# Layer 0's first products taken by sequence tile over all row blocks in eight PSUM banks, all in rounded parts; an own chain for the first tile; another order and other queues for the last half's stores

## The chip, the cores and the metric

The kernel runs on one core of one Trainium2 chip. The core has five engines that run side by side and meet through semaphores: TensorE (PE; PEld is its weight load), VectorE (DVE), ScalarE (ACT), GpSimd (POOL) and SyncE (SP), which here only issues DMAs. All DMAs, whichever engine issues them, are carried by the core's 16 DMA engines. The metric is the device time of one execution in microseconds (us), as the median of several runs.

## The reference

The model alternates two layers, twice. Layers 0 and 2 are a Fourier mixing layer, layers 1 and 3 a gated feed-forward layer; each is added to its input. Sequence length S is 2048, width D is 512, hidden width F is 1792, all in float32.

```python
def _A_ref(x, dft_seq_re, dft_seq_im, dft_hid_re, dft_hid_im):
    a = jnp.einsum("bsd,ed->bse", x, dft_hid_re)
    b = jnp.einsum("bsd,ed->bse", x, dft_hid_im)
    return jnp.einsum("ts,bse->bte", dft_seq_re, a) - jnp.einsum("ts,bse->bte", dft_seq_im, b)
def _B_ref(x, w_gate, w_up, w_down):
    return (_gelu(x @ w_gate) * (x @ w_up)) @ w_down
x = A_x
x = x + _A_ref(_layernorm(x), ...)
x = x + _B_ref(_layernorm(x), ...)
x = x + _A_ref(_layernorm(x), ...)
x = x + _B_ref(_layernorm(x), ...)
```

## The kernel before

**Products.** A float32 product is made of three faster matmuls. Each operand is divided into a rounded high part (ACT copies it into the type float32r) and the low rest (DVE subtracts the high part from the value); `split` does this (L115 to L117). `mm3` (L148 to L152) then adds high by high, high by low and low by high into one PSUM bank. A plain float32 matmul is used in one place only, below.

**Mixing layer.** The product with the sequence matrices comes first. The sequence is cut into four row blocks `b` of 512 output rows and 16 sequence tiles of 128 input rows; the matrix pieces `ws` are 128 by 512 and 256 KB each. Real and imaginary part form a 2 by 2 block product in Strassen's manner with seven products per row block, named A11, A12, S2, S1, S3, S4, A22. Each product runs over `NK` = 8 tiles, with two column halves `c`, so one product of one row block is 8 x 2 x 3 matmuls. `plan` (L387) lists the stages. In layer 0 the two products A11 (tiles 0 to 7 of the normalized rows, left half) and A12 (tiles 8 to 15) of all four row blocks come first: A11 for b = 0, 1, 2, 3, then A12 for b = 0, 1, 2, 3, each in two banks of its own. The remaining products of block 0 follow (S2 with S1 and S3, then S4 with A22), each with products by the hidden matrices between, then those of blocks 1, 2 and 3.

**A11 and A12.** `a11` (L733) asks `bare` (L400) whether it is layer 0, block 0. There the raw piece `t` is multiplied with the normalized row `za[k]` by two plain float32 matmuls (L739), without dividing either. Otherwise `six` (L716) takes the divided piece from the stream and makes six matmuls. At the end of A11 both banks are copied by ACT into `sums[b]`. `a12` (L750) then adds `sums[b]` and its own banks on DVE into `t`; for blocks 1 to 3 both are put away in DRAM through POOL's queue (`put_away`, L235).

**The stream.** `items` is the list of all pieces in the order of use. `load_next` (L272) issues a load on SP; `split_next` and `take` (L297) keep up to `AHEAD` = 7 pieces divided before their use (more where `stream["more"]` is set), and `RAW` = 6 loaded ahead of that. `step` (L464), called after each group of matmuls, runs one entry of `queue`; that is how normalizing and dividing the rows is laid between products. A scheduler of the framework then sets the order of instructions on each engine.

**The opening** (L1265 to L1304). `WARM` = 16 small matmuls of the identity run first (L1267). Four rows tiles `x` and four pieces are loaded in turn, and rows 0 and 1 are normalized at once (`first_norm`, `norm_terms` L482: DVE takes `bn_stats`, `bn_aggr` and adds EPS, POOL raises to -0.5 at L497, DVE makes `shift`, and ACT applies scale and shift at L526). `queue` then holds the other rows of the first half with `first_parts` (the divided left half), then `second_norm` and `second_parts` for rows 8 to 15, then `combine` and `combine_late`, which make the sums of halves that S2 and the later products need. Working tiles come from a pool of `NSLOT` = 94 slots of 128 by 512; `norm_terms` of layer 2 takes one as a place for an output that nobody reads (`junk`).

**The end** (L1231 to L1254). The last half block of layer 3 runs its down products in the order of `down_order` (L407), where the products S3 are spread between S4, and both end at about the same time. Then `last_rows` (L1193) makes A22 in two cuts of 256 columns. After each cut DVE transposes and adds into a wide tile (`turned_rows`, L220), and four stores of 128 KB go out, two from SP and two from ACT (L1209). The rows of the neighbouring group, 1 MB, are stored by POOL when S4 is done (`rows_done`, L230, issued at L231).

Of the kernel before, what the change touches and what calls it, by code (L numbers as in the profile page):

```python
# [2 lines left out]

# [50 lines left out]
def fnet_geglu(ctx: ExitStack, tc: tile.TileContext, x_in, ws, wh, whc, wgu, wdc, out):  # L54
# [15 lines left out]
    nc.vector.memset(warm, 0.0)  # L70
    nc.scalar.activation(warm, warm, AF.Gelu_apprx_tanh)

    power = cpool.tile([P, 1], F32, name="power")
    nc.vector.memset(power, -0.5)

# [37 lines left out]
        return ap.bitcast(F32)  # L113

    def split(src, hi, lo):  # L115
        nc.scalar.activation(hi, src, AF.Copy)  # L116
        nc.vector.tensor_tensor(lo, src, f32(hi), op=ALU.subtract)  # L117

    def split_slot(src):
        hi, lo = sb.get(F32R), sb.get(F32R)  # L120
# [193 lines left out]

    s1s, s2s, s3s, cs, held = {}, {}, {}, {}, {}

    def as_is(v):
        return (v,)

    def whole(*parts):  # L320
        return parts

# [64 lines left out]
    def plan(layer):  # L387

        fore, steps = FORE[layer], []
        steps += [(b, "A11") for b in range(fore)] + [(b, "A12") for b in range(fore)]  # L390
# [9 lines left out]
    def bare(layer, b, what):  # L400

        return layer == 0 and b == 0 and what == "A11"
# [12 lines left out]

    def mix_items(layer):
        def raw(make, *tiles):
            items.append((F32, tiles, make, None))

        for b, what in plan(layer):  # L420
            tiles = [[ws[(b * 2 + m) * NS + k] for k in range(NS)] for m in range(2)]
            (a11, a12), (a21, a22) = ((r[:NK], r[NK:]) for r in tiles)
            hold = b >= FORE[layer]
            if what == "A11":
                for k in range(NK):
                    raw(as_is if bare(layer, b, what) else make_a11(k) if hold else plain, a11[k])
            elif what == "A12":
                for k in range(NK):
                    raw(plain, a12[k])
            elif what == "S2":  # L430
                for i, k in skewed(3):
                    if i == 0:
                        raw(make_s2(k, b in KEEP22[layer]), a21[k], a22[k], *(() if hold else (a11[k],)))
                    else:
                        raw(make_s1(k) if i == 1 else make_s3(k))
            elif what == "S4":
                for i, k in skewed(2):
                    if i == 0:
                        raw(make_s4(k), a12[k])
                    elif b in KEEP22[layer]:  # L440
                        raw(make_a22(k))
                    else:
                        raw(plain, a22[k])
            elif what == "PAIR":
                for name, k in PAIR_ORDER:
                    items.append((F32R, (piece_of(whd, k, name),), whole, NEAR_PAIR))
            else:
                for m, c in what:
                    if layer == 0 and b == 0:
                        items.append((F32, (wh[m * ND + c],), make_hid_first(m, c), (m, c)))  # L450
                    else:
                        items.append((F32R, halves(whs[m, c]), make_hid(m, c), (m, c)))

    for layer in range(0, 4, 2):
        mix_items(layer)
        for w in range(NB // 2):
            for near, products in zip(NEAR, down_order()):
# [54 lines left out]
    def terms_ahead(layer, i, n):  # L512

        if i == 0:
            fresh["terms"] = x_load(layer, 0)
        x, junk = fresh.pop("terms"), sb.get()
# [3 lines left out]
        sb.put(x, junk)  # L520

    def normed(layer, i, mixed=False):
        x = row_of(layer, i, mixed)
# [151 lines left out]
    def mix(layer):  # L675
# [57 lines left out]
        def a11(b):  # L733
            chain = [ps8.get() for _ in range(2)]
            for k in range(NK):
                if bare(layer, b, "A11"):
                    t, = take()
                    for c in range(2):
                        nc.tensor.matmul(chain[c], za[k][:, c * P:(c + 1) * P], t, start=k == 0, stop=k == NK - 1)  # L739
# [10 lines left out]
        def a12(b):  # L750
# [4 lines left out]
            for c in range(2):  # L755
# [9 lines left out]
                else:  # L765
                    plus(v, v, side[c])
                    cs[0, c] = v
            ps8.put(*side)

        chains, sides, us, later = {}, {}, {}, {}  # L770

# [142 lines left out]
        for n, (b, what) in enumerate(plan(layer)):  # L914
            if n == len(plan(layer)) - 1:
# [2 lines left out]
                    weight_load(1)  # L918
                while queue:
                    step()  # L920
            if what in stages:
                stages[what](b)
                if what == "S4":
                    pair_member(b)
# [82 lines left out]
    def geglu(w, layer):  # L1007
# [185 lines left out]
        def last_rows():  # L1193
# [40 lines left out]
        late = down_order()[1]  # L1234
        last = layer == 3 and w == 1
        if last:
            late = late[:-NP]
        for i, (name, k) in enumerate(late):
# [35 lines left out]
            loaded.add(i)  # L1274
            fresh[i] = x_load(0, i)

    for i in range(4):
        x_ahead(i)
        load_next()

    def opening(k):

        def run():
            x_ahead(k + 2)
            if k < NK:
                first_norm(0, k)
            first_parts(k - 2)
        return run

    def second_opening(k):  # L1290
        def run():
            x_ahead(NK + k + 2)
            second_norm(0, k)
        return run

    first_norm(0, 0)
    first_norm(0, 1)
    queue.extend(opening(k) for k in range(2, NK + 2))
    for k in range(NK):
        queue += [second_opening(k), lambda k=k: second_parts(k), *([None] if k % 2 else [])]  # L1300
    for k in range(NK):
        queue += [lambda k=k: combine(k), None]
    for k in range(NK):
        queue += [lambda k=k: combine_late(k), None]  # L1304

    for layer in range(4):
        if layer % 2 == 0:
# [70 lines left out]
```

## Time and profile before

| what | value |
|---|---|
| runs | 1599.57 us median of 3 (1598.54 to 1601.11) |
| the profiled execution: its own time | 1600.61 us |
| its span, first to last instruction | 1598.8 us |
| granted TensorE clock over the span, mean | 0.999 |
| DVE / ACT / POOL busy | 77% / 53% / 14% of the span |
| DMA moved | 422.86 MB, mean 264 GB/s |

The profile is taken from one execution. A row of the timeline gives start and duration in us, engine, line, operation, what is written from what, and in brackets the idle time before it with what ended it. A row of the windows gives, for a stretch, the busy us of each engine with the number of instructions that touch it, the granted clock, the busy share of the DMA engines and GB/s. A group row gives a count, the total busy time and the mean ns of one. One plain float32 matmul shows as two records, and a float32r matmul as one. The records of successive matmuls overlap, so what a matmul costs TensorE is the distance between two starts, not its duration; the same holds for long rows of like instructions on DVE and ACT.

### The profile page before, as it was taken

The numbers are of one execution on the slowest core, as the hardware profiler recorded it, in microseconds if no ns is written. First come the engines' busy times: TensorE is split into PE (matmuls) and PEld (weight loads), VectorE is DVE, ScalarE is ACT, GpSimd is POOL, SyncE is SP. The second block draws the span as 40 slices with busy tenths as digits, with TensorE's granted clock in tenths as the row PEclk, the third lists the DMA queues.
The fourth block names the chain that finished last, engine by engine and source line by source line (L and its number), as shares of the span: only waits on it lengthen the run. The fifth ranks groups of instructions, "written<-read, shape, count | busy, mean of one in ns | idle before, by whom it ended". The sixth has DMA issues, their size and how long they took to land.

```text
span 1598.8 us, 23037 instructions
## 1 busy us (share of the span) xinstructions
PE 1588.5 (99%) x7018; PEld 1312.4 (82%) x7018; DVE 1236.6 (77%) x2148; ACT 846.0 (53%) x1664; POOL 219.5 (14%) x409
## 2 busy tenths in 40 slices
PE   9999999999999999999999999999999999999997
PEld 6888888888888888888888888888888888888886
DVE  7999989689789795665969987789985548754484
ACT  7754464445677653556777534536446535433360
POOL 2112210211455201220041000001001000000000
PEclk9999999999999999999999999999999999999999
DMA  9869986787999999995867777886998967996462
GB/s 359 292 207 329 357 269 223 247 282 253 346 342 342 308 310 306 307 350 195 274 233 255 238 261 228 273 267 211 260 341 240 292 190 227 314 283 197 126 191 53
DMA packets 276604, 422.86 MB, mean 264 GB/s; under 512 B 28864, under 2 KB 131520, under 8 KB 275456
## 3 DMA queue, kind: packets, MB, share of 16 engines
q1 hardware_dynamic: 251600, 338.26, 66.8%
q0 software_dynamic: 23792, 82.59, 14.0%
q8 instruction: 56, 0.92, 0.2%
q10 hardware_dynamic: 1088, 0.52, 0.1%
q14 instruction: 68, 0.56, 0.1%
HBM read 339.74 MB, written 81.53 MB: 263 GB/s over the span
## 4 chain that ended last, share of the span: by engine, by line
PE 95%; DMA 3%; DVE 1%; SPq 1%; issue 0%; ACT 0%; POOL 0%; POOLq 0%; ACTq 0%
PE p L150 31%; PE p L151 31%; PE p L152 31%; DMA s<-x 1%; PE p L739 1%; DMA s<-wh 1%; SPq L187 1%; DMA xwide<-x 1%; DMA s<-wb 1%; PE p L1267 0%; DVE s L117 0%; DVE s L138 0%; ACT s L504 0%; SPq L944 0%; DVE s L134 0%
## 5 line engine op out<-in xcount | busy, mean ns | idle before, releaser
L151 PE MATMUL p<-s,s 128*128 128x512 f32 (+1 forms) x2318 | 897.0, 388 | 0.0
L152 PE MATMUL p<-s,s 128*128 128x512 f32 (+1 forms) x2318 | 892.2, 388 | 0.0
L150 PE MATMUL p<-s,s 128*128 128x512 f32 (+1 forms) x2318 | 873.3, 389 | 0.4 <-ACT s L145 0.4
L116 ACT ACTIVATE s<-s 128x512 fp32r<-128x512 f32 (+1 forms) x828 | 464.6, 606 | 350.9 <-DVE s L138 144.5
L117 DVE TENSOR_TENSOR s<-s,s 128x512 fp32r<-128x512 f32 (+1 forms) x828 | 518.5, 660 | 56.5 <-ACT s L116 54.2
L150 PEld LDWEIGHTS p<-s,s 128*128 128x128 f32 x2318 | 435.4, 188 | 91.6 <-ACT s L145 1.3
L152 PEld LDWEIGHTS p<-s,s 128*128 128x128 f32 x2318 | 435.4, 188 | 89.9 <-issue 0.5
L151 PEld LDWEIGHTS p<-s,s 128*128 128x128 f32 x2318 | 435.4, 188 | 89.6 <-issue 0.7
L141 DVE TENSOR_TENSOR s<-s,p 128x512 f32<-128x512 f32 x291 | 194.9, 681 | 195.7 <-PE p L152 109.9
L138 DVE TENSOR_TENSOR s<-s,s 128x512 f32<-128x512 f32 (+1 forms) x408 | 246.3, 618 | 11.3 <-DMA s<-ws 9.0
L145 ACT ACTIVATE s<-p 128x512 f32<-128x512 f32 x240 | 140.5, 591 | 145.8 <-PE p L152 141.4
L1004 ACT ACTIVATE s<-s 128x512 f32<-128x512 f32 x112 | 70.2, 629 | 118.2 <-DVE s L141 116.8
L507 POOL TENSOR_SCALAR rstd<-rstd 128x1 f32<-128x1 f32 x48 | 16.6, 346 | 342.2 <-ACT s L506 333.4
L1018 DVE TENSOR_TENSOR s<-s,s 128x512 f32<-128x512 f32 x84 | 57.8, 688 | 1.9
L265 POOL DMA_DIRECT2D wb<-s x84 | 45.4, 543 | 91.7 <-ACT s L116 71.1
L116 ACT ACTIVATE s<-xwide 128x512 fp32r<-128x512 f32 (+1 forms) x66 | 39.7, 616 | 24.2 <-DVE xwide L138 13.8
L526 ACT ACTIVATE s<-s,shift,rstd 128x512 f32<-128x512 f32 x61 | 48.8, 807 | 6.9 <-DVE shift L498 6.6
L141 DVE TENSOR_TENSOR s<-s,s 128x512 f32<-128x512 f32 (+1 forms) x70 | 41.6, 597 | 12.0 <-issue 5.4
L117 DVE TENSOR_TENSOR s<-xwide,s 128x512 fp32r<-128x512 f32 (+1 forms) x66 | 44.1, 674 | 5.6 <-ACT s L116 5.5
L231 POOL DMA_DIRECT2D out<-wide x8 | 5.2, 655 | 290.4 <-DVE wide L141 184.3
L504 ACT ACTIVATE s<-s 128x512 f32<-128x512 f32 x45 | 28.0, 622 | 30.6 <-DMA s<-x 28.8
L231 POOL DMA_DIRECT2D x<-wide x12 | 7.8, 660 | 237.3 <-DVE wide L141 168.7
(105 smaller groups left out, 530.0 us busy)
## 6 DMA issues: line engine op xcount, KB each, us to landing
s<-ws SPq DMA_DIRECT2D x364, 256.0 KB, 5.0
s<-wb SPq DMA_DIRECT2D x294, 256.0 KB, 5.4
s<-wc SPq DMA_DIRECT2D x196, 256.0 KB, 4.3
wb<-s POOLq DMA_DIRECT2D x98, 256.0 KB, 6.0
s<-wh SPq DMA_DIRECT2D x85, 256.0 KB, 5.3
xwide<-ws SPq DMA_DIRECT2D x55, 256.0 KB, 4.2
s<-x SPq DMA_DIRECT2D x54, 256.0 KB, 4.7
wc<-s POOLq DMA_DIRECT2D x49, 256.0 KB, 5.6
```

Source lines behind the costliest of these rows:

```text
L116: nc.scalar.activation(hi, src, AF.Copy)
L117: nc.vector.tensor_tensor(lo, src, f32(hi), op=ALU.subtract)
L138: nc.vector.tensor_tensor(out, a, b, op=ALU.subtract)
L141: nc.vector.tensor_tensor(out, a, b, op=ALU.add)
L145: nc.scalar.activation(v, src, AF.Copy)
L150: nc.tensor.matmul(ps, ah, bh, start=start, stop=False, skip_group_check=True)
L151: nc.tensor.matmul(ps, ah, bl, start=False, stop=False, skip_group_check=True)
L152: nc.tensor.matmul(ps, al, bh, start=False, stop=stop, skip_group_check=True)
L265: nc.gpsimd.dma_start(a, f32(t))
L526: nc.scalar.activation(z, x, AF.Identity, bias=shift, scale=rstd)
L1004: nc.scalar.activation(t, g, AF.Gelu_apprx_tanh)
L1018: nc.vector.tensor_tensor(t, t, v, op=ALU.mult)
```

## The change

- `plan` puts one stage FORE in the place of the eight stages A11 and A12 in layer 0. The new function `fore` holds all eight PSUM banks, two for each row block, and goes over the 16 sequence tiles; within a tile it makes the six matmuls of each of the four row blocks. After tile 7 the banks are copied into `sums[b]` and the accumulation goes on in the same banks; after tile 15 they are copied again. A12's addition on DVE is gone, and the plain float32 product with it. The pieces `ws` are loaded in the order of use, by tile.
- The opening loads x0, two pieces, x1, two pieces, x2. `first_tile` handles row tile 0: it subtracts the mean on DVE, lets ACT round the scaled left half straight from that, and DVE make the rest; the whole normalized row is made later, by ACT. While it runs, the divisions of the first pieces are ordered behind this chain. The other rows are interleaved by `OPEN_GAPS` and `SECOND_AT`.
- `WARM` goes from 16 to 12. `junk` gets a tile of its own and `NSLOT` goes from 94 to 93.
- In the last half block all S3 products come before the last five S4 products, and the second cut's four stores go out over SP, ACT and POOL (then SP again).

```diff
-WARM = 16
+WARM = 12
+OPEN_MORE = 0
+SECOND_AT = 2
+OPEN_GAPS = 1, 2, 1, 1, 1, 1, 1
-NSLOT = 94
+NSLOT = 93
...
     def split(src, hi, lo):
-        nc.scalar.activation(hi, src, AF.Copy)
-        nc.vector.tensor_tensor(lo, src, f32(hi), op=ALU.subtract)
+        with behind(0):
+            nc.scalar.activation(hi, src, AF.Copy)
+        with behind(1):
+            nc.vector.tensor_tensor(lo, src, f32(hi), op=ALU.subtract)
...
-    def down_order():
+    def down_order(last=False):
...
-        for k in range(2, NP):
-            late += [("S3", 3 * (k - 2) // 2 + i) for i in range(1 + k % 2) if 3 * (k - 2) // 2 + i < NP] + [("S4", k)]
+        if last:
+            late += [("S3", k) for k in range(NP)] + [("S4", k) for k in range(2, NP)]
+        else:
+            for k in range(2, NP):
+                late += [("S3", 3 * (k - 2) // 2 + i) for i in range(1 + k % 2) if 3 * (k - 2) // 2 + i < NP] + [("S4", k)]
...
+            if what == "FORE":
+                for j in range(NS):
+                    for c in range(FORE[layer]):
+                        raw(plain, ws[c * 2 * NS + j])
+                continue
...
-                if bare(layer, b, "A11"):
-                    t, = take()
-                    for c in range(2):
-                        nc.tensor.matmul(chain[c], za[k][:, c * P:(c + 1) * P], t, start=k == 0, stop=k == NK - 1)
-                    sb.put(t)
-                    step()
-                else:
-                    six(chain, "B11", k, k == 0, k == NK - 1, "11" if b == NB - 1 else None)
+                six(chain, "B11", k, k == 0, k == NK - 1, "11" if b == NB - 1 else None)
...
+        def fore(n):
+            banks = [[ps8.get() for _ in range(2)] for _ in range(n)]
+            for j in range(NS):
+                name, k = ("B11", j) if j < NK else ("B21", j - NK)
+                for b in range(n):
+                    six(banks[b], name, k, j == 0, k == NK - 1, name[1:] if b == n - 1 else None)
+                    if k < NK - 1:
+                        continue
+                    if j < NK:
+                        sums[b] = [copied(p) for p in banks[b]]
+                        continue
+                    stream["more"] = 0
+                    for c, p in enumerate(banks[b]):
+                        t = copied(p)
+                        ps8.put(p)
+                        if b:
+                            put_away((layer, b, c), sums[b][c])
+                            put_away((layer, b, c, "sum"), t)
+                        else:
+                            cs[0, c] = t
...
-            for cut, engines in ((slice(0, CUT), (nc.sync, nc.scalar)), (slice(CUT, TB), (nc.sync, nc.scalar))):
+            for cut, engines in ((slice(0, CUT), (nc.sync, nc.scalar)), (slice(CUT, TB), (nc.sync, nc.scalar, nc.gpsimd))):
...
-    for i in range(4):
-        x_ahead(i)
-        load_next()
+    x_ahead(0)
+    load_next()
+    load_next()
+    x_ahead(1)
+    load_next()
+    load_next()
+    x_ahead(2)
...
+    def first_tile():
+        x, st, mv, rstd = fresh.pop(0), *(spool.tile([P, n], F32, name=name) for name, n in (("st", 6), ("mv", 2), ("rstd", 1)))
+        nc.vector.bn_stats(st, x)
+        nc.vector.bn_aggr(mv, st)
+        nc.vector.tensor_scalar_add(rstd, mv[:, 1:2], EPS)
+        nc.gpsimd.tensor_tensor(rstd, rstd, power, op=ALU.pow)
+        nc.vector.tensor_scalar(x, x, mv[:, 0:1], None, op0=ALU.subtract)
+        split_next()
+        p = zparts["11", 0] = sb.get(F32R)
+        high = nc.scalar.activation(p[:, half[0]], x[:, half[0]], AF.Copy, scale=rstd)
+        made = nc.vector.scalar_tensor_tensor(p[:, half[1]], x[:, half[0]], rstd, f32(p[:, half[0]]), op0=ALU.mult, op1=ALU.subtract)
+        terms_made.append((made.ins, made.ins))
+        first_made.extend((high.ins, made.ins))
+        split_next()
+        split_next()
+        first_made.clear()
+        def whole_row():
+            z = za[0] = sb.get()
+            nc.scalar.activation(z, x, AF.Copy, scale=rstd)
+            sb.put(x)
+        return whole_row
...
+    firsts = [run for k in range(1, NK) for run in (opening(k), lambda k=k: first_parts(k))]
+    seconds = [run for k in range(NK) for run in (second_opening(k), lambda k=k: second_parts(k))]
+    sums = [run for k in range(NK) for run in (lambda k=k: combine(k), lambda k=k: combine_late(k))]
+    for n in range(NK - 1):
+        queue += [firsts.pop(0), firsts.pop(0)]
+        queue += [seconds.pop(0) if n >= SECOND_AT else None for _ in range(OPEN_GAPS[n])]
+    queue += seconds
+    queue.append(later_row)
+    for run in sums:
+        queue += [run, None]
```

More of the change, by code (lines that the diff above doesn't have):

```diff
@@ L389, in plan @@
         fore, steps = FORE[layer], []
-        steps += [(b, "A11") for b in range(fore)] + [(b, "A12") for b in range(fore)]
+        if layer == 0:
+            steps += [(None, "FORE")]
+        else:
+            steps += [(b, "A11") for b in range(fore)] + [(b, "A12") for b in range(fore)]
         for b in range(NB):
@@ L425, in mix_items @@
                 for k in range(NK):
-                    raw(as_is if bare(layer, b, what) else make_a11(k) if hold else plain, a11[k])
+                    raw(make_a11(k) if hold else plain, a11[k])
             elif what == "A12":
@@ L456, in fnet_geglu @@
         for w in range(NB // 2):
-            for near, products in zip(NEAR, down_order()):
+            for near, products in zip(NEAR, down_order(layer == w * 2 == 2)):
                 for name, k in products:
@@ L920, in mix @@
                     step()
-            if what in stages:
+            if what == "FORE":
+                fore(FORE[layer])
+            elif what in stages:
                 stages[what](b)
@@ L1233, in geglu @@
         pair_combined(NP - 1)
-        late = down_order()[1]
         last = layer == 3 and w == 1
+        late = down_order(last)[1]
         if last:
@@ L1291, in run @@
         def run():
-            x_ahead(NK + k + 2)
+            x_ahead(NK + k + 1)
             second_norm(0, k)
         return run
[L1296 to L1304, printed above, removed]
+    def first_tile():
[17 more added lines that the diff above has]
+            nc.scalar.activation(z, x, AF.Copy, scale=rstd)
+            sb.put(x)
+        return whole_row
+    later_row = first_tile()
+    stream["more"] = OPEN_MORE
+    firsts = [run for k in range(1, NK) for run in (opening(k), lambda k=k: first_parts(k))]
[8 more added lines that the diff above has]
+        queue += [run, None]
     for layer in range(4):
```

22 lines of the change are left out of this document (11 added, 11 removed).

## The prediction

> **What bounds the kernel now.** I read the page first, then windows over its parts, then the timelines of the opening and of the end. Of the page the span, the engines and the chain of waits:
>
> ```profile
> span 1598.8 us, 23037 instructions
> PE 1588.5 (99%) x7018; PEld 1312.4 (82%) x7018; DVE 1236.6 (77%) x2148; ACT 846.0 (53%) x1664; POOL 219.5 (14%) x409
> PE 95%; DMA 3%; DVE 1%; SPq 1%; issue 0%; ACT 0%; POOL 0%; POOLq 0%; ACTq 0%
> ```
>
> TensorE holds 95% of the chain that sets the end. A busy share can hide slack, so I count starts. The window of a quiet stretch, and the list of who waited for whom on PE:
>
> ```profile
> 1200.00:1400.00 200.00, 200.00 (x884) 165.69 (x883) 125.66 (x200) 101.11 (x202) 12.49 (x27) 1.00 0.83 252
> PE p L1267 <- POOL ident masks.py:199: 1.4, 1, 1.4
> PE p L150 <- ACT s L145: 0.4, 1, 0.4
> ```
>
> 884 matmuls touch 200 us; one straddles an edge, so a step is 200/883 = 0.2265 us, at full granted clock (1.00), and TensorE waits once for 0.4 us after its start. So time comes only from three places: a different sum of matmul steps, the stretch before the first product, and the stretch after the last matmul. The change touches all three, and it can open new waits.
>
> **Part 1: the plain float32 product goes.** The timeline of PE where it stands in a row:
>
> ```profile
> 7.82 5.32 PE L739 MATMUL p<-s,s 128*128 128x512 f32 x12
> L739 PE MATMUL p<-s,s 128*128 128x512 f32 x32 | 14.7, 592 | 0.0
> ```
>
> Twelve records fill 5.32 us and the last lasts 0.59, so eleven steps take 4.73 us, 0.43 each. 32 records (16 matmuls, two records each) are 32 x 0.43 = 13.8 us of TensorE. They become 8 tiles x 2 halves x 3 = 48 float32r matmuls: 48 x 0.2265 = 10.9 us. This lies on the path: minus 2.9 us.
>
> Dividing the eight raw pieces is new: eight more copies on ACT and eight subtractions on DVE. A12's closing additions (two for each of four blocks, 128x512, on DVE) go, and eight copies on ACT replace them, so DVE has as many instructions as before and ACT 16 more. The windows of the stages concerned (columns PE, PEld, DVE, ACT, POOL):
>
> ```profile
> 7.80:34.50 26.70, 26.70 (x91) 16.68 (x90) 23.83 (x69) 21.80 (x42) 5.53 (x10) 1.00 1.05 386
> 60.00:100.00 40.00, 40.00 (x179) 33.12 (x178) 40.00 (x75) 24.91 (x45) 2.20 (x4) 1.00 0.78 255
> 100.00:133.00 33.00, 33.00 (x147) 27.36 (x146) 33.00 (x56) 16.40 (x28) 3.78 (x7) 1.00 0.55 189
> ```
>
> ACT has 15 us free of 40 after 60 us, so its 16 operations cost nothing there. DVE is full from 60 to 133 us while PE never waits; it runs ahead of PE by its store of divided pieces. PE now comes to this stretch about 3 us sooner with the same DVE work before it, which uses up lead and no more; I cost it at 0, and at 2 us if the lead were gone.
>
> The copies after tile 7 stand between a bank's last matmul of tile 7 and its first of tile 8. The other three row blocks, 18 matmuls or 4.1 us, cover two copies of 0.6 us each. Cost 0.
>
> **Part 2: the start.** The windows of the warm-up's weight loads and matmuls alone, and the timeline around it:
>
> ```profile
> 1.30:6.90 5.60, 5.55 (x26) 5.55 (x27) 1.00 0.85 295
> 6.90:7.75 0.85, 0.85 (x8) 0.85 (x7) 1.00 1.01 328
> ...
> 3.45 0.69 DVE L493 BATCH_NORM_STATS2 st<-s 128x6 f32<-128x512 f32 x1 [2.56 <-DMA s<-x]
> 4.18 0.18 DVE L495 BATCH_NORM_AGGREGATE mv<-st 128x2 f32<-128x6 f32 x1
> 4.40 0.15 DVE L496 TENSOR_SCALAR rstd<-mv 128x1 f32<-128x1 f32 x1
> 4.63 0.56 POOL L497 TENSOR_TENSOR rstd<-rstd,power 128x1 f32<-128x1 f32 x1 [3.34 <-DVE rstd L496]
> 5.42 0.81 ACT L526 ACTIVATE s<-s,shift,rstd 128x512 f32<-128x512 f32 x1 [3.20 <-DVE shift L498]
> 6.27 0.42 ACT L116 ACTIVATE s<-s 128x256 fp32r<-128x256 f32 x1
> 7.58 0.42 DVE L117 TENSOR_TENSOR s<-s,s 128x256 fp32r<-128x256 f32 x1
> ```
>
> The first row is normalized at 5.42 + 0.81 = 6.23 us, yet the first product starts at 7.82: the warm-up is last there. 16 warm matmuls show as 32 records; some 26 take 5.6 us (0.21 each), the last take 0.85 us for about eight (0.106 each); the granted clock reads 1.00 in both, so the pace is read from the counts. Four fewer take away eight records. [...] At the slow pace it would be 8 x 0.21 = 1.7 us, the far bound; the near bound is 0, if an operand is late.
>
> The operand: the mean's subtraction on DVE isn't in this trace in that shape; the nearest row is 0.42 us for half a tile, so up to 0.7 for a whole one, beside the 0.56 us of POOL. From 5.2 us ACT rounds the half tile (0.42): ready at 5.6, its rest by 6.1. The first piece now is the second load instead of the third. [...]
>
> [...]
>
> **Part 3: feeding tile by tile.** A tile is 24 matmuls, 5.44 us, and needs four pieces and one new row tile with its whole chain. The loads, and the timeline where ACT and DVE divide pieces in a row:
>
> ```profile
> s<-ws SPq DMA_DIRECT2D x30, 256.0 KB, 5.4
> 11.25 3.00 ACT L116 ACTIVATE s<-s 128x512 fp32r<-128x512 f32 x6
> 11.89 3.44 DVE L117 TENSOR_TENSOR s<-s,s 128x512 fp32r<-128x512 f32 x6 [0.53 <-ACT s L116]
> ```
>
> At 386 GB/s (the window 7.80 to 34.50) a 256 KB load takes 0.68 us of the queue; four pieces and two row tiles are 4.1 us of a tile's 5.44. On SP the order changes: before, x3 was the sixth load; now it stands behind 17 pieces and three row tiles, as the 21st. The second load has landed by 4.48, when DVE takes row 1 right after row 0, so the 21st lands near 4.5 + 19 x 0.68 = 17.4 to 18 us. From there the chain is 0.69 + 0.18 + 0.15 + 0.55 + 0.15 + 0.81 + 0.42 = 3 us, and what is queued ahead of it on DVE, four divisions at (3.44 - 0.68)/5 = 0.55, adds 2.2: ready at about 23. [...] I take 0.7 us of stalls in tiles 1 to 5, between 0 and 2.5: what is late next is the tile's low part, which the scheduler lays behind 16 other matmuls of the tile, 3.6 us of cover.
>
> A slot fewer, the own `junk` tile and the opening's other entries add no instruction to a full engine: 0.
>
> **Part 4: the end.** The timeline of the last 20 us and windows of the same place:
>
> ```profile
> 1578.20 1.37 DVE L141 TENSOR_TENSOR s<-s,p 128x512 f32<-128x512 f32 x2 [11.13 <-PE p L152]
> 1580.05 0.28 PE L150 MATMUL p<-s,s 128*128 128x256 f32 x1
> 1580.12 0.65 DVE L141 TENSOR_TENSOR s<-s,p 128x512 f32<-128x512 f32 x1
> 1584.30 0.41 DVE L225 STREAM_TRANSPOSE s<-p 128x256 f32<-128x256 f32 x1
> 1584.63 1.25 DVE L141 TENSOR_TENSOR wide<-wide,s 128x512 f32<-128x512 f32 x2
> 1586.13 0.44 DVE L225 STREAM_TRANSPOSE s<-p 128x256 f32<-128x256 f32 x1
> 1586.17 2.57 POOL L231 DMA_DIRECT2D out<-wide  x4 [184.32 <-DVE wide L141]
> 1587.06 6.13 SPq L1209 DMA_DIRECT2D out<-xwide  x4
> 1590.00 0.28 PE L152 MATMUL p<-s,s 128*128 128x256 f32 x1
> 1590.80 0.42 DVE L141 TENSOR_TENSOR xwide<-xwide,s 128x256 f32<-128x256 f32 x1
> ...
> 1588.00:1592.00 4.00, 2.28 (x19) 2.07 (x18) 1.55 (x4) 0.00 (x0) 0.74 (x2) 1.00 0.95 222
> 1592.00:1597.50 5.50, 0.00 (x0) 0.00 (x0) 0.00 (x0) 0.00 (x0) 0.00 (x0) 0.72 0.78 195
> 1597.50:1598.80 1.30, 0.00 (x0) 0.00 (x0) 0.00 (x0) 0.00 (x0) 0.00 (x0) 0.50 0.00 0
> ...
> DMA to landing us min/median/max: 3.1/5.7/7.9
> ```
>
> The last matmul ends at 1590.28, the data are in place at 1591.22, and the span ends 7.6 us later. The DMA engines are 95% busy from 1588 on: 2 MB (POOL's 1 MB, eight stores of 128 KB) go out in a row, so the last stores wait behind the earlier ones. S3's six DVE operations (1578.20 on) and S4's six (1580.12 on) share 7.7 us of DVE. With S3 done five products sooner, only S4's six follow 1580.12, at 0.6 each: 3.7 us. POOL's stores then go at about 1583.9 instead of 1586.17, and the first cut's, which wait for their second half on PE (84 matmuls in 10 us make 0.12 each, so 42 end near 1585.1), at about 1586.2 instead of 1587.06. At 222 GB/s the first 1.5 MB need 7 us, from 1585 to 1592, so the last 0.5 MB, issued at 1591.25 as before, find the queue nearly empty. A store that does lands after 3.1 us (the least in the last row); the other three at 222 GB/s add at most 1.8. I take 4.4 of these 3.1 to 4.9: 1595.7, where the DMA engines now fall silent at 1597.5. I take minus 1.8 us, between minus 2.5 and plus 0.5: the third queue may cost, since POOL's four issues take 2.57 us and its stores land no sooner than SP's.
>
> [...]
>
> **The sum.** -2.9 - 0.85 + 0.7 - 1.8 = -4.85 us. Against the profiled execution's own 1600.61 us (span 1598.8 and 1.8 around it) that is 1595.8; this execution lies 1.0 over the median of the runs, so I predict 1594.7. With all bounds at their good ends -2.9 - 1.7 - 0 - 2.5 = -7.1, 1592.5; at their bad ends -2.9 - 0 + 2.5 + 2 + 0.5 = +2.1, 1601.7.
>
> **The rivals.** *A. DVE becomes the bound of the opening (slower).* The groups of the first 40 us:
>
> ```profile
> L117 DVE TENSOR_TENSOR s<-s,s 128x512 fp32r<-128x512 f32 x19 | 12.7, 683 | 1.1 <-ACT s L116 0.8
> L493 DVE BATCH_NORM_STATS2 st<-s 128x6 f32<-128x512 f32 x14 | 9.6, 688 | 3.5 <-DMA s<-x 3.5
> L117 DVE TENSOR_TENSOR s<-s,s 128x256 fp32r<-128x256 f32 x16 | 6.4, 413 | 0.8 <-ACT s L116 0.8
> ```
>
> From tile 3 each tile carries four divisions, a first row (0.69 + 0.18 + 0.15 + 0.15 + 0.41) and a second row (1.17 + 2 x 0.41). At mean durations that is 2.73 + 1.58 + 1.99 = 6.3 us against 5.44: 0.86 over in each of about eight tiles, 7 us, and 1594.7 + 7 = 1601.7. It decides as soon as a DVE operation costs more than 5.44/6.3 = 0.86 of its duration. Against it: the six divisions in a row cost 0.55 of 0.68, a ratio of 0.81, which makes 5.1 us. The margin is thin, and it can be eaten by waits in DVE's order, where an operation with a late row holds up the divisions behind it.
>
> *B. The matmuls are saved, the rest is given back.* Stalls of 2.2 us for x1, x3 and x5, and an end that stays: -2.9 - 0.85 + 2.2 = -1.55, 1598.0. For it: x3's load as the 21st, and DVE's strict order. Against it: loads are faster than use from the first tile on.
>
> *C. All goes well.* No stall, the slow pace for the four warm-ups or an end 2.5 us shorter: about -6.5, 1593.1.
>
> *D. The change does little:* the matmul sum is arithmetic on counts, so this can only be B carried further, and is in it.
>
> **How the numbers follow.** The forecast has 0.62 (its own range 1593.3 to 1596.8), C 0.12, B 0.14, A 0.12. A measurement of this kernel can tell about 0.2%, 3.2 us, from no change; faster therefore ends at 1596.4 and slower begins at 1602.8. A's price is uncertain around 1601.7; as it feeds on itself once begun (a late tile delays the next), I put two thirds of it past 1602.8. Faster: C and the forecast but its edge, 0.72. Within 0.2%: that edge, B and a third of A, 0.20. Slower: 0.08. The range 1592.0 to 1599.0 takes in the forecast, B and most of C and leaves out A.
>
> **What would show it.** Right: no record of a plain float32 product; the first product near 6.95 us; 24 matmuls in each 5.44 us from there, with gaps of 0.7 us in sum before 45 us; PE without a wait from 45 to 400 us; POOL's stores about 6.4 us before the last matmul ends, instead of 4.1; from the last matmul to the end 6.7 us instead of 8.5. Wrong: PE waiting for DVE in every tile from 3 on (A), waits of 2 us and more at x1, x3 or x5 with 8.5 us at the end (B), or waits at the change from layer 0's stage to S2 near 95 us, which would say that DVE's lead was smaller than I take it.

## The result, and the profile after

| | median us | lowest to highest | runs | profiled run | span |
|---|---|---|---|---|---|
| before | 1600.70 | 1598.54 to 1602.51 | 19 | 1600.61 | 1598.8 |
| changed | 1602.78 | 1600.44 to 1605.86 | 19 | 1600.54 | 1598.8 |

The ratio is 1.0014, with a 95% interval of 1.0007 to 1.0020: 2 us slower, where 5 us less were predicted. The profiled execution of the changed kernel is one of its fastest: its span equals that of before, so the two traces show where the gain went; the further 2 us of the median belong to other executions.

The page of the changed kernel, its span, engines and chain of waits:

```profile
span 1598.8 us, 23017 instructions
PE 1586.9 (99%) x7026; PEld 1313.1 (82%) x7026; DVE 1236.8 (77%) x2148; ACT 856.4 (54%) x1680; POOL 225.2 (14%) x410
PE 83%; issue 12%; DMA 3%; ACT 1%; POOL 1%; DVE 0%; SPq 0%; POOLq 0%; ACTq 0%; DVEq 0%
```

The chain looks far worse than before's 95% on PE, but it misleads: the fastest kernel below has "PE 84%; issue 12%" too. What tells is who waited for whom on PE, in the changed kernel (total us, times, longest):

```profile
PE p L161 <- ACT s L156: 1.5, 2, 1.1
PE p L1298 <- POOL ident masks.py:199: 1.4, 1, 1.4
PE p L162 <- DVE s L123: 1.1, 2, 0.8
PE p L161 <- ACT s L121: 0.5, 2, 0.3
```

Before had one wait of 0.4 us after the start. The view counts only waits that it can put down to a releaser. From the starts in the trace, every step above 0.24 us less 0.2267, I count after 45 us 1.0 us of lost TensorE time in before and 4.95 in the changed kernel: 1.8 at 184 to 189 us, 1.3 at 477 and 1.5 at 662 to 668. Below, "lost" is this count.

The opening, in timelines of PE and DVE:

```profile
1.35 5.49 PE L1298 MATMUL p<-ident 128*128 128x128 f32 x24 [1.35 <-POOL ident masks.py:199]
4.44 0.48 DVE L1338 TENSOR_SCALAR s<-s,mv 128x512 f32<-128x512 f32 x1
6.49 0.77 PE L161 MATMUL p<-s,s 128*128 128x512 f32 x1
7.06 0.55 PE L162 MATMUL p<-s,s 128*128 128x512 f32 x1
7.45 0.40 PE L161 MATMUL p<-s,s 128*128 128x512 f32 x1
23.84 0.50 PE L161 MATMUL p<-s,s 128*128 128x512 f32 x1 [0.29 <-ACT s L121]
```

No plain float32 product is left. The first product starts at 6.49; its first two steps take 0.57 and 0.39 in place of 0.23, so it is worth a start at 7.0. From there to 45 us TensorE loses 0.8 us, most of it at 23 us, where the rounding of row 3 is awaited: x3's load has landed at 17.97, but its statistics start only at 19.67, when nine divisions that stand before them on DVE are done.

The end, in timelines and windows:

```profile
1584.75 2.56 POOL L242 DMA_DIRECT2D out<-wide  x4 [182.22 <-DVE wide L152]
1587.35 5.84 SPq L1240 DMA_DIRECT2D out<-xwide  x4
1591.13 0.28 PE L163 MATMUL p<-s,s 128*128 128x256 f32 x1
1588.00:1592.00 4.00, 3.41 (x29) 3.20 (x27) 1.40 (x4) 0.00 (x0) 0.00 (x0) 1.00 0.98 229
1592.00:1597.50 5.50, 0.00 (x0) 0.00 (x0) 0.35 (x1) 0.00 (x0) 0.58 (x1) 0.73 0.56 145
```

The last matmul ends at 1591.41, 7.4 us before the span does (8.5 before); POOL's stores go 6.7 us before that end (4.1 before).

So all three stretches that were meant to gain did. The balance of the two traces: -2.9 for the product's matmuls, -0.8 for the start, +0.8 of waits in the opening, +3.95 of waits after it (4.95 less 1.0) and -1.1 at the end, 0.0 in all. The whole question is the 3.95.

### The profile page after: what moved, and what is told of

It is laid out like the page before. It is cut to its first block, busy times and chain, and to the rows that moved or that the text cites. A ratio compares the mean times of both kernels' runs of the same rounds, so it can differ in the third digit from the quotient of the medians.

```text
span 1598.8 us, 23017 instructions
## 1 busy us (share of the span) xinstructions
PE 1586.9 (99%) x7026; PEld 1313.1 (82%) x7026; DVE 1236.8 (77%) x2148; ACT 856.4 (54%) x1680; POOL 225.2 (14%) x410
## 4 chain that ended last, share of the span: by engine, by line
PE 83%; issue 12%; DMA 3%; ACT 1%; POOL 1%; DVE 0%; SPq 0%; POOLq 0%; ACTq 0%; DVEq 0%
PE p L162 28%; PE p L161 28%; PE p L163 28%; DMA s<-ws 2%; POOL rstd L521 0%; DMA wide<-x 0%; DMA s<-x 0%; ACT s L121 0%; DMA s<-wdc 0%; SPq L293 0%; ACT s L540 0%; DVE s L123 0%; DVE s L152 0%; POOL out L242 0%; ACT s L156 0%
## 5 line engine op out<-in xcount | busy, mean ns | idle before, releaser
L149 DVE TENSOR_TENSOR s<-s,s 128x512 f32<-128x512 f32 (+1 forms) x403 | 242.3, 617 | 7.2 <-DMA s<-ws 4.9
L156 ACT ACTIVATE s<-p 128x512 f32<-128x512 f32 x246 | 143.8, 592 | 142.2 <-PE p L163 141.3
L1035 ACT ACTIVATE s<-s 128x512 f32<-128x512 f32 x112 | 70.1, 629 | 120.8 <-DVE s L152 120.1
L152 DVE TENSOR_TENSOR s<-s,s 128x512 f32<-128x512 f32 (+1 forms) x69 | 40.2, 586 | 15.6 <-DMA s<-ws 6.1
L624 DVE STREAM_TRANSPOSE wide<-s 128x512 f32<-128x512 f32 x31 | 21.8, 705 | 20.3 <-ACT s L540 17.6
```

The costliest lines, as they stand in the source:

```text
L149: nc.vector.tensor_tensor(out, a, b, op=ALU.subtract)
L152: nc.vector.tensor_tensor(out, a, b, op=ALU.add)
L156: nc.scalar.activation(v, src, AF.Copy)
L1035: nc.scalar.activation(t, g, AF.Gelu_apprx_tanh)
```

## The experiments

The theories. **S:** the slots. 93 in place of 94, or the statistics' scratch tile of its own (S1 and S2 below), make the build lay out ACT's, DVE's and SP's operations in another order through the whole program, and the new waits come from that. **G:** TensorE arrives earlier in the stretch of 140 to 200 us, where the DMA engines are full, and gives its gain back there. **C:** chance. S fits the order of the two programs: the sequence of operations (by operation, tile names and shapes in the traces of before and changed) differs at 180 places on ACT and 219 on DVE, from start to end. G fits the windows of the changed kernel (the last two columns are the DMA engines' busy share and GB/s):

```profile
140.00:200.00 60.00, 58.92 (x258) 47.72 (x257) 55.08 (x97) 29.52 (x55) 17.72 (x33) 1.00 0.97 361
400.00:600.00 200.00, 198.95 (x878) 164.39 (x877) 170.63 (x310) 128.02 (x258) 71.39 (x124) 1.00 0.94 320
600.00:700.00 100.00, 99.31 (x436) 81.19 (x435) 58.01 (x98) 50.12 (x114) 23.10 (x44) 1.00 1.00 305
700.00:1000.00 300.00, 300.00 (x1325) 248.40 (x1324) 243.50 (x424) 177.89 (x354) 31.23 (x58) 1.00 0.76 255
```

All three places lie where the DMA share is 0.94 or more; where it is 0.76, PE loses nothing.

### First set: the change taken apart

*94 slots again, scratch from a slot* (the changed kernel else):

```
-NSLOT = 93
+NSLOT = 94
-        x = fresh.pop("terms")
+        x, junk = fresh.pop("terms"), sb.get()
-        sb.put(x)
+        sb.put(x, junk)
```

> The changed kernel with 94 slots again and the statistics' scratch taken from a slot as before; opening and end as changed. Theory S (fewer slots and a scratch tile of its own put the ACT and DVE operations of the whole program in another order, and the new TensorE waits at 184-189, 477 and 662-668 us come from that): these waits are gone, TensorE waits less than 1.5 us between 45 and 1560 us, and the time is 4 to 6 us under the kernel before, about 1595 to 1597. Rival G (TensorE arrives some 4 us earlier in the stretch of 140 to 200 us that the DMA engines fill, and gives the opening's gain back there): the wait near 184 us stays, of 1.5 us or more, and the time is within 2 us of the changed kernel, 1600 to 1603. Rival C (waits that fall by chance in any order): new waits of 2 to 5 us in other places, 1598 to 1603.

*The kernel before with 93 slots and its own scratch tile*, the reverse of that edit on before:

> The kernel before with 93 slots and a scratch tile of its own, nothing else. Theory S: slower than before by the waits that the changed kernel has, 4 to 6 us, with TensorE waits of over 1 us in some places between 100 and 700 us: 1604 to 1607. Rival G: as before, within 1 us, since TensorE arrives nowhere earlier: 1600 to 1601.5. Rival C: slower than before by 0 to 4 us.

*Without the new end* (the changed kernel with before's `down_order` and two store queues):

> The changed kernel with the end of the kernel before (last half's order and stores undone). All theories agree that the end is worth what the two traces show for it, 1.15 us from the last product to the end of the program: 0.8 to 2 us slower than the changed kernel, some 1604; the tail after the last product is 8.5 us again, and the waits at 184-189, 477 and 662-668 us stay, since the order up to there is the changed kernel's. If these waits move or vanish, they are chance and not order.

*The new end alone* on the kernel before:

> The kernel before with the changed end alone. Both theories: 1 to 1.8 us faster than before, some 1599, the tail after the last product 7.4 us or less in place of 8.5. If the end has done nothing: within 0.5 us of before.

| kernel | slots | opening | end | median us | ratio to before, 95% interval | lost after 45 us |
|---|---|---|---|---|---|---|
| before | 94 | old | old | 1600.33 | | 1.0 |
| new end alone | 94 | old | new | 1598.72 | 0.9991, 0.9982 to 1.0000 | 0.2 |
| 94 slots | 94 | new | new | 1595.68 | 0.9972, 0.9962 to 0.9983 | 0.8 |
| before with 93 | 93 | old | old | 1603.70 | 1.0026, 1.0015 to 1.0037 | 4.2 |
| without new end | 93 | new | old | 1604.28 | 1.0029, 1.0018 to 1.0039 | 5.7 |
| changed (from the result) | 93 | new | new | 1602.78 | 1.0014, 1.0007 to 1.0020 | 4.95 |

S holds. One edit that adds no operation to PE, ACT or DVE turns 1.0014 into 0.9972, 6.7 us, and costs the kernel before 4 us by itself (1603.70 lies 0.3 under the range expected of S and inside that of C). The order does change with it: the kernel before and the same with 93 slots differ at 166 places on ACT and 221 on DVE, from 24 us on. Who waited on PE with 94 slots and the new opening and end (its lines stand one lower):

```profile
span 1594.5 us, 23082 instructions
PE p L1297 <- POOL ident masks.py:199: 1.3, 1, 1.3
PE p L160 <- ACT s L120: 0.7, 2, 0.4
PE p L160 <- DVE s L1048: 0.2, 1, 0.2
```

The two ACT waits are in the opening, at 12.7 and 24.3 us. G alone falls: at 140 us this kernel has 6422 matmuls left to start, the changed kernel 6420 and before 6432, so it comes there as early, and it loses nothing. Nor does the edit alone lose there: before with 93 slots has its waits at 479 and 664 to 670 us and none at 184. With 93 slots and the new opening together all three appear. Chance falls too: the same places come back in every kernel of that order, and with 94 slots no more than 0.7 us is lost at any of them.

The end by itself: its two kernels with 94 slots take 6.9 us from the last matmul's end to the span's end, so it is worth 1.6; the pair with 93 slots shows 1.5 (8.9 against 7.4).

### Second set: the slots or the tile, and the wait at 477 us

*94 slots with the tile of its own*, the one line `NSLOT = 94` in the changed kernel:

> The changed kernel with 94 slots in place of 93, the statistics' scratch tile of its own kept. Theory S1 (the number of slots does it: with one more, buffers are reused later and the operations fall in another order): as with 94 slots and the scratch from a slot, 1595 to 1597, TensorE waits after 45 us under 1.5 us in all, and no wait at 477 and 662-668 us. Rival S2 (the scratch tile of its own does it): as the changed kernel, 1602 to 1604, with these waits.

*93 slots with the scratch from a slot*:

> The changed kernel with 93 slots, but the statistics' scratch taken from a slot as before, so that it has 93 buffers in all where the changed kernel has 94. Theory S1: the waits of the changed kernel or more, 1602 to 1606. Rival S2: as with 94 slots and the scratch from a slot, 1595 to 1597.

Measured: 1596.27 us (0.9970, 0.9959 to 0.9981) and 1602.42 us (1.0017, 1.0008 to 1.0026), with 6.4 us lost after 45 us in the second. It is the number of slots, S1; the tile changes the order in a few places between 630 and 710 us, and the time by no more than the intervals show. A further execution of the first, for its trace:

> The changed kernel with 94 slots and the scratch tile of its own once more, for its trace: about 1596, TensorE waits after 45 us under 1.5 us in all, none over 0.3 us at 177-190, 477 and 655-668 us.

1595.62 us, 0.5 us lost after 45 us, and one wait of PE after the start:

```profile
span 1593.7 us, 23076 instructions
PE p L1298 <- POOL ident masks.py:199: 1.4, 1, 1.4
PE p L161 <- ACT s L121: 0.4, 1, 0.4
```

And the changed kernel itself a second time:

> The changed kernel itself once more, for a second trace. All theories: TensorE waits in the same places as in the first (177-190, 477, 655-668 us), 4.5 to 8 us in all after 45 us; the size at 177-190 and 655-668 us, where a DMA's landing decides, differs by up to 2 us from the first, the one at 477 us, where GpSimd waits for VectorE, does not.

1601.65 us, 5.4 lost: 1.5 at 184 us (1.8 in the first trace), 1.33 at 477 (1.32) and 2.5 at 662 to 669 (1.5). As expected; the order on ACT, DVE, POOL and SP is the same in both traces to the last operation.

The wait at 477 us can be read from the timelines of the changed kernel:

```profile
471.74 4.72 POOL L521 TENSOR_SCALAR rstd<-rstd 128x1 f32<-128x1 f32 x1
471.79 0.68 DVE L149 TENSOR_TENSOR s<-s,s 128x512 f32<-128x512 f32 x1
...
475.40 1.01 DVE L149 TENSOR_TENSOR s<-s,s 128x256 f32<-128x256 f32 x2
476.55 0.56 POOL L522 TENSOR_TENSOR rstd<-rstd,power 128x1 f32<-128x1 f32 x1
477.14 0.29 ACT L523 ACTIVATE shift<-mean,rstd 128x1 f32<-128x1 f32 x1 [3.17 <-POOL rstd L522]
478.57 0.57 ACT L156 ACTIVATE s<-p 128x512 f32<-128x512 f32 x1
479.20 0.50 PE L161 MATMUL p<-s,s 128*128 128x512 f32 x1 [1.05 <-ACT s L156]
```

A multiply-and-add on 128 numbers, 0.19 us in the median of 48, takes 4.72. DVE runs operations with two SBUF operands (`s<-s,s`) end to end from 471.79 to 476.41, and POOL's ends at 476.46. ACT waits for the result in its order, its copy of a PSUM bank (L156) comes late, and PE waits for the bank. The kernel before has one such operation as well (312.22 us, until DVE's pause at 315.9); ACT waits 2.84 us for its row there, but PE loses nothing:

```profile
312.22 3.77 POOL L507 TENSOR_SCALAR rstd<-rstd 128x1 f32<-128x1 f32 x1 [21.60 <-ACT s L506]
```

Theory P says that POOL waits for DVE; Q, that this operation alone was slow. Two kernels alter the one row tile in question, the fourteenth statistics made on ACT:

```
+            acts.append(i)
+            if len(acts) == 14:
+                nc.scalar.activation(rstd, rstd, AF.Copy, scale=1.0 / D, bias=EPS)
+            else:
+                nc.gpsimd.tensor_scalar(rstd, rstd, 1.0 / D, EPS, op0=ALU.mult, op1=ALU.add)
```

> The changed kernel, for one row tile alone (the one whose statistics take 4.72 us on GpSimd at 471.74 us): the multiply-and-add of its 128x1 statistics runs on ACT, the power stays on GpSimd. Theory P (GpSimd's small operations wait for as long as VectorE runs operations with two SBUF operands back to back, here until 476.4 us): the power now waits in its place, 4 us or more from 472 us, ACT's wait for it and the TensorE wait of 1 us or more near 477 us stay. Rival Q (the multiply-and-add alone was slow): the power takes 0.6 to 1.1 us, no TensorE wait near 477 us, about 1.3 us less in the span.

> As the kernel with the multiply-and-add on ACT, but the power of this one row tile is left out as well: its scale is set to the constant 0.05 on ACT, so this row's result is not the reference's. Both theories: no TensorE wait near 477 us, about 1.3 us less in the span than the changed kernel's 1598.8. If the wait stays, neither holds, and ACT's copy is late for another reason.

The first, 1603.63 us, in timelines of POOL, DVE and ACT:

```profile
472.98 2.91 POOL L526 TENSOR_TENSOR rstd<-rstd,power 128x1 f32<-128x1 f32 x1 [0.79 <-ACT rstd L523]
474.79 0.69 DVE L123 TENSOR_TENSOR s<-s,s 128x512 fp32r<-128x512 f32 x1
475.93 0.29 ACT L527 ACTIVATE shift<-mean,rstd 128x1 f32<-128x1 f32 x1 [1.80 <-POOL rstd L526]
```

The power, 0.56 us in the median elsewhere, now takes 2.91 and ends 0.4 us after DVE's run does (474.79 + 0.69 = 475.48). So P holds and Q falls, but the sizes missed: ACT now waits sooner, and in ACT's queue behind this wait stood the rounding that DVE needed next, so DVE's run broke off earlier and let POOL in. PE lost nothing there. In the changed kernel's trace POOL's operation did not get in between the eight instructions of DVE's run (471.79 to 476.41) either, and took 4.72 us. What in DVE's run kept it out, the place of the operands or something else, was not tried.

In the second, 1603.62 us, the wait at 477 us is gone, as both theories had it; yet neither kernel became faster, by one execution each. They lost 7.7 and 7.5 us after 45 us, 5.3 and 4.3 of it at 660 to 670. That wait had grown.

### Third set: how the number matters

*Nine more warm-up products* (`WARM = 21`, 93 slots):

> The changed kernel with 21 warm-up products in place of 12, so that the first product starts 9 x 0.43 = 3.9 us later; 93 slots. Rival G, for what it still can hold (with 93 slots TensorE's earlier arrival in the full DMA stretch costs the waits at 177-190 us, which the old opening with 93 slots does not have): these waits fall under 0.6 us, and the time is 3.9 - 1.8 = 2 us over the changed kernel, 1604 to 1605.5. If the arrival has no part in it: the waits there stay at 1.5 us or more, 1606 to 1608.

*92 slots* (`NSLOT = 92`):

> The changed kernel with 92 slots. Theory S1 read as room (each slot fewer lets the loads run less far ahead where the DMA engines are full): slower than with 93 slots, 1604 to 1612, with TensorE waits of more than 5 us after 45 us, in the same stretches (140-200, 400-600, 600-700 us). Read as order alone (any other number is another order, good or bad): anything from 1596 to 1606, the waits in other places, also in stretches where the DMA engines have room.

The first: 1601.18 us (1.0009, 1.0000 to 1.0018). Both expectations missed, since the delay was mis-sized. Timeline of PE:

```profile
1.35 7.75 PE L1298 MATMUL p<-ident 128*128 128x128 f32 x42 [1.35 <-POOL ident masks.py:199]
8.85 0.47 PE L161 MATMUL p<-s,s 128*128 128x512 f32 x1
```

Eighteen more records take 7.75 - 5.49 = 2.26 us, 0.126 each and not 0.215, so the first product came 2.36 us later and not 3.9. And the delay cost next to nothing (a span of 1599.1 against 1598.8), for the slow first steps (0.5 us) and the opening's waits (0.8 us) vanish, and 1.0 is lost at 180 to 190 us in place of 1.5 to 1.8. What is left of G, that earliness matters at 184 us once the order is bad, is neither shown nor refuted.

92 slots: 1597.30 us (0.9982, 0.9973 to 0.9991), 2.1 us lost, almost all at 655 us. One slot less than 93 is 5 us faster, so it is not room that 93 slots lack: the number picks an order, and 93 picked a bad one. The expectation by room fell.

### Fourth set: the waits at 655 to 669 us

There ACT sat 5.35 us for a row, in the changed kernel's timeline, while DVE waited for a piece of the weights `whc`:

```profile
660.94 0.63 ACT L518 ACTIVATE junk<-s 128x512 f32<-128x512 f32 x1 [5.35 <-DMA s<-x]
662.30 0.43 DVE L152 TENSOR_TENSOR s<-s,s 128x256 f32<-128x256 f32 x1 [4.54 <-DMA s<-whc]
668.48 0.50 PE L161 MATMUL p<-s,s 128*128 128x512 f32 x1 [0.47 <-ACT s L156]
```

The view names the row. Theory R takes it at its word; D holds that the full DMA engines and SP's queue are behind it. The statistics made ahead read a constant tile `still` in place of the row, first with the loads kept:

```
-        known[layer, i] = norm_terms(layer, i, x, junk)
+        known[layer, i] = norm_terms(layer, i, still, junk)
```

> The changed kernel, 93 slots; the eight statistics made ahead for the second layer's first rows (630 to 695 us) read a constant tile in place of the row loaded for them (the loads stay, the results of these rows are not the reference's), so that ACT has no row to wait for there. Theory R (ACT waits in order for the row, and the PSUM copies and splits behind it come late): TensorE waits under 0.6 us in all at 640-680 us, the ones at 177-190 and 477 us stay, 1.5 to 3 us less than the changed kernel, 1599 to 1601. Rival D (the full DMA engines hold TensorE there by other loads): 1.5 us or more of waits stay at 640-680 us, the time within 1 us of the changed kernel.

> As the kernel before it, and the one row tile at 472 us has its scale set to the constant 0.05 on ACT, with nothing of it on GpSimd. Theory R: waits under 0.6 us at 640-680 us and none at 477 us; left is 177-190 us, 1.5 to 2.6 us: 1598 to 1599.5. Rival D, or waits that move on when they are taken away in one place: 3 us or more of waits after 470 us, 1600 or more.

Measured: 1604.98 us (1.0027, 1.0016 to 1.0038) and 1602.83 us (1.0014, 1.0004 to 1.0023). At 660 to 680 us 5.3 and 7.3 us are lost, more than ever. R falls; D missed the first one's time, which it had within 1 us of the changed kernel. Timelines of ACT, DVE, PE and SP of the first:

```profile
657.45 0.33 SPq L976 DMA_DIRECT2D s<-whc  x1
665.02 0.63 ACT L122 ACTIVATE s<-s 128x512 fp32r<-128x512 f32 x1 [5.31 <-DMA s<-whc]
667.76 0.43 DVE L153 TENSOR_TENSOR s<-s,s 128x256 f32<-128x256 f32 x1 [7.32 <-DMA s<-whc]
670.11 0.80 PE L162 MATMUL p<-s,s 128*128 128x512 f32 x1 [3.45 <-DVE s L153]
```

With no row to wait for, ACT and DVE wait for `whc`. Its first load is issued at 657.45 and lands at 665.00. So, for D, the same kernel with the eight row loads left out too (their slots are taken and given back):

```
-            fresh["terms"] = x_load(layer, i + 1)
+            fresh["terms"] = sb.get()
```

> As the kernel with the constant tile in place of the rows, and the eight row loads (128x512 float32, 0.26 MB each, 2.1 MB at 620 to 690 us) left out as well, so that SP's queue and the DMA engines have so much less to do there. Theory D (DMA engines that are full from 600 to 700 us, and loads that lie behind others, hold TensorE): the loads of whc land 3 to 7 us earlier, TensorE waits under 1 us in all at 640-680 us, 4 to 6 us less than with the constant tile alone (1604.98), 1599 to 1601. If these waits stay at 3 us or more: not the DMA engines, but the order of SP's queue or of ACT and VectorE holds it.

1600.55 us (1.0000, 0.9991 to 1.0010): 4.4 less than with the loads. In its timelines and a window:

```profile
653.21 0.33 SPq L976 DMA_DIRECT2D s<-whc  x1
661.01 0.43 DVE L153 TENSOR_TENSOR s<-s,s 128x256 f32<-128x256 f32 x1 [4.82 <-DMA s<-whc]
660.00:680.00 20.00, 19.44 (x85) 15.42 (x84) 15.27 (x28) 8.93 (x17) 4.93 (x9) 1.00 0.92 317
```

The first load of `whc` goes 4.2 us sooner and lands at 658.93, 6.1 sooner; 0.9 us are lost at 660 to 680. D holds: other loads hold `whc` back in this stretch, where the DMA share is 1.00 to 1.03 in the window 600 to 700 us of these two kernels, of before, of the changed one and of that with 94 slots. Whether it is their place in SP's queue or their traffic was not separated, since the edit takes away both. With 94 slots the first load of `whc` goes at 639.99, before at 644.71, in the changed kernel at 648.90; but that load alone does not decide, for with 93 slots and the scratch from a slot it goes at 642.51, its third only at 656.68, and 2.3 us are lost at 640 to 660. Which buffer or wait puts these loads later with 93 slots was not followed further.

The wait at 184 us, the largest of the three in the first trace (1.8 us), was not taken away by itself. DVE stands there for a load too, of a piece `ws`; with 94 slots (scratch from a slot) its longest wait for one there is 1.46 us, and PE loses nothing. Timeline of the changed kernel:

```profile
183.54 0.69 DVE L152 TENSOR_TENSOR s<-s,s 128x512 f32<-128x512 f32 x1 [3.11 <-DMA s<-ws]
```

Both kernels with 94 slots and the new opening and end beat the kernel before and the changed one: 1595.68 and 1596.27 us, 4.5 and 4.8 us under before by their ratios.

## Why the prediction was wrong, point by point

- **The step that failed** is "A slot fewer, the own `junk` tile and the opening's other entries add no instruction to a full engine: 0." The premise is true and the conclusion is not. By the ratios it costs 6.7 us with the new opening and 4.2 without. With 93 slots the build lays out another order on ACT, DVE and SP; the new order puts POOL's statistics under a run of DVE (1.3 us at 477 us), and the loads of `whc` behind others (1.5 to 2.5 at 662 to 669). At 184 us (1.5 to 1.8) the trace shows a late load as well, but no run tried it. How one slot less leads to this order, by way of the buffer that a load gets and the time it may go, was not followed, so this link is argued and not shown. The tile of its own is worth 0, as said.
- **The rest of the sum** can be tried on the kernel with 94 slots, since it is the change without this edit. It gives -4.5 by its ratio (predicted -4.85) and 1595.68 against the forecast of 1594.7. By its trace: -2.9 from the counts; the first product worth a start near 6.8 where 6.95 was predicted and before has 7.8, so -1.05 for -0.85; 1.5 us of waits in the opening for 0.7, within 0 to 2.5; 0.2 less lost after 45 us; 1.6 at the end for 1.8. The sum is -4.25, and the spans differ by 4.3. That the terms agree so well is in part luck: the opening varies from one execution to the next. Before's opening starts its first product at 7.82 us, and at 7.03 in the kernel with the new end alone; the changed kernel's at 6.49, and at 5.98 in its second trace, where it loses 2.45 us to 45 us in place of 1.3. The late row was read rightly: x3 lands at 17.97, within the predicted 17.4 to 18.
- **The warm-up's price.** The sum's -0.85 takes the eight records left out at 0.106 us each, my estimate from the pace of before's last eight. No run shows this term by itself, nor the 0.7 us of stalls: the runs showed a start worth 7.0 in the changed kernel (-0.8) and near 6.8 with 94 slots (-1.05), with 0.8 and 1.5 us of waits in the opening behind it. The pace was near for these traces: before's 32 records take 6.63 us, the changed kernel's 24 take 5.49 (0.14 for each of the eight), and eighteen more took 0.126 us each. It is no constant: in the changed kernel's second trace the same 24 records take 4.29 us, and in the kernel with the new end alone 32 take 5.84.
- **ACT's and DVE's new operations** cost 0 in layer 0, as predicted: with 94 slots no more than 0.2 us is lost from 45 to 400 us. The lead of DVE held.
- **The rivals.** A (DVE the bound of the opening) gives 1601.7, near the result, but for a reason that did not happen: no wait grew from tile to tile. B had the gain given back by x1, x3 and x5 and an end that stays; the opening gave back 0.8 and the end gained. The real rival, an order that is worse far from the edit, was not among them, although the 0.4 us of waits on PE in before could have told that another order had nearly nothing to gain and much to lose.
- **What would show it** did its work: "PE without a wait from 45 to 400 us" failed at 184 us.

## What to carry to other kernels

A buffer count is not a cost of nothing where a build lays out the order from it: compare the orders of both kernels on every engine, and where they differ far from the edit, price the difference by the waits that a busy stretch has room for, or keep the count (here 94 slots and the extra tile fitted together). In a stretch where the DMA engines are full (a share of 1.00 and more here), the releaser that the profile names may be only the last of several late ones; take it away by itself before believing it.

## What the runs showed of the hardware

**A long wait of TensorE cost again after it had ended.** In the kernel with the multiply-and-add on ACT, PE lost 3.5 us at 662 us. Its timeline after the wait, and windows of PE alone (the columns after its busy time and count are granted clock, DMA share and GB/s):

```profile
665.77 0.88 PE L161 MATMUL p<-s,s 128*128 128x512 f32 x2 [3.35 <-ACT s L121]
667.09 0.63 PE L163 MATMUL p<-s,s 128*128 128x512 f32 x1
660.00:665.00 5.00, 2.41 (x11) 1.00 0.86 270
665.00:670.00 5.00, 4.23 (x11) 0.66 0.76 259
670.00:672.00 2.00, 2.00 (x11) 1.00 0.73 275
```

From 667.09 to 669.22 the steps are 0.43 us, the granted clock of the window 665 to 670 is 0.66, and 1.2 us more are lost. The kernels with the constant tile show the same after losses of 3.6 and 5.4 us: the granted clock is 0.50 at 670 to 672 us in both. In the kernel where the whole statistic is a constant on ACT it was 0.50 too, at 667 to 670 us, after a loss of 2.4 us with three of 0.1 to 0.2 right behind it. In the changed kernel, which loses 1.5 us at 662 to 668 us, it is 1.00 in each window from 655 to 675 us. The slower steps made those executions longer than their waits, and may be part of why the runs with 93 slots spread over 5.4 us (1600.44 to 1605.86) and those with 94 over 2.5 (1595.15 to 1597.64); that was not tried.

**A small operation on POOL waited for a whole run of DVE**: 4.72 us for 0.19 us of work at 471.74 in the changed kernel (4.73 in its second trace, and 4.73 in the kernel before with 93 slots), 3.77 at 312.22 in before.
